# The MLP's second layer with activations as weights, and a scatter by blocks of 128 rows

## The chip, the cores and the metric

The kernel runs on one core of one Trainium2 chip. The metric is the device time of one execution in microseconds; lower is better. A profiled execution has a span, which goes from its first to its last instruction.

## What is computed

The reference has three stages in a row (cut to what matters):

```python
# attention: q, k, v [4, 12, 448, 64], RMS norm of q and k, softmax
# its output becomes x: 1792 tokens x 768
# moe: 8 experts, each takes 224 tokens; assignment is greedy over sorted logits
for e in range(E):
    h = np.maximum(x[mask] @ w1[e], 0.0)      # 768 -> 1024
    out[mask] = h @ w2[e]                     # 1024 -> 768
# cos MLP on all 1792 tokens
h = x @ w_in                                  # 768 -> 2048
g = h * np.cos(h)
return (g @ w_out).astype(np.float32)         # 2048 -> 768
```

`w_in` and `w_out` come as 64-bit floats. The kernel narrows them on the chip to pairs of 32-bit parts (hi, lo), which TensorE multiplies as float32r.

## The kernel before

**Order of work.** Every operation is put as a step into a `Plan` (lines 52 to 260), with the engines it may run on and an assumed cost; `Plan.run` then simulates the engines, chooses among available steps by due time (`late`, lowered by `rush`), and emits the program in that order. So a change of steps also changes the order of the others. A second plan, begun after the attention, holds the experts and the MLP.

**Routing.** Experts are found one after the other. `Router.phase` (line 1045) gives for one expert `idx`, a [112, 2] tile with the token numbers of its 224 rows in two halves, by products of one-hot rows `oh` with the digits `pv` of the token number (three digits, added by a reduce). For the third expert on it uses a search (`slow`, line 1003): SyncE writes `rows`, reads it back in eight broadcasts into `AB` (line 1014), and eight rounds of VectorE and TensorE (`ind`, `bd`) follow. GpSimd then gathers the expert's rows by an indirect DMA (line 1182).

**Groups.** Experts are taken in four pairs, `GROUPS`. For each pair both experts run, and leave 448 columns of activations, feature by feature, in `x2h` and `x2l`; then `mlp` (line 1304) does both layers for these 448 tokens. The route of the next pair's first expert is entered in the plan (`ahead`) in the middle of the second layer.

**MLP.** Layer one: 16 feature blocks f, each 6 x 3 matmuls of 448 columns (`three`: hi by hi, hi by lo, lo by hi), then the cosine on ScalarE and VectorE into `gh` and `gl`. Layer two: 6 output blocks d of 128 features, each 16 x 3 matmuls of 448 columns with w_out as weights. The result lies feature by feature, so ScalarE copies it to `o`, TensorE transposes it in four pieces of 112 tokens (into `tr`), VectorE copies these into `xo`, and after the last d four indirect DMAs (`scatter`, line 1349) write 112 rows each to the tokens' places, with `idx`. In the last group the last d is done in two halves of 224 columns. Weights come as 1 MB pieces through a ring of four buffers `wx` (`ready`, line 1236), all issued by SyncE (`SP`), which also issues the expert weights and the router's DMAs in program order.

**Narrowing.** `Narrow` (line 270) cuts w_in into 32 pieces and w_out into 24. 48 are narrowed during the attention and written to `w_in32`, `w_out32`; the last 8 of w_out, those of d = 4 and 5, are narrowed in group 0's second layer (`fresh`, line 1243), through `ws` and `na` into `wx`, and written out for the later groups.

Of the kernel before, what the change touches and what calls it, by code (L numbers as in the profile page):

```python
# [12 lines left out]
F32 = mybir.dt.float32  # L13
# [256 lines left out]
class Narrow:  # L270

    WIDE = {"wi": 3, "wo": 4}

    def __init__(self, nc, pairs):

        self.nc = nc
        self.todo, self.at = [], {}
        for tag, src, dst in pairs:
            s = src.bitcast(I32)
            for f in range(dst.shape[0]):  # L280
                n = self.WIDE[tag]
                for k in range(0, dst.shape[2], n):
                    w = s[k * 128:(k + n) * 128, f * 256:(f + 1) * 256].rearrange("(k p) c -> p k c", p=128)
                    self.at[tag, f, k] = len(self.todo)
                    self.todo.append((w, dst[f, :, k:k + n], f"{tag}{f}:{k}"))

    def piece(self, plan, i, raw, mag, parts=None):

        nc, v = self.nc, plan.vector
        src, dst, name = self.todo[i]  # L290
        n = dst.shape[1]
        r, a = raw[:, 0:n], mag[:, 0:n]
# [3 lines left out]
        plan.add([("SP", 0.46, lambda: nc.sync.dma_start(r, src))], [], [r], dma=0.36 * n, land=LAND)  # L296
# [7 lines left out]
        plan.add([("SP", 0.46, lambda: nc.sync.dma_start(dst, o.bitcast(F32)))], [o], [name], dma=0.36 * n)  # L304

    def plan(self, plan, pool, last):

        most = max(self.WIDE.values())
        raw = plan.ring(pool)("nr", 4, [128, most, 256], I32)
        mag = plan.ring(pool)("na", 2, [128, most, 128], I32)  # L310
        for i in range(last):
            self.piece(plan, i, raw(), mag())
# [412 lines left out]
class Router:  # L725
# [3 lines left out]
    def __init__(self, nc, pool, ident, L, rows):  # L729
# [76 lines left out]
        v.tensor_copy(io, tmp[0:CP, 272:272 + CP])  # L806
        pc = t("pc", [CP, NCOL, 3], BF16)
# [237 lines left out]
    def phase(self, idx, eid, first, quick):  # L1045
# [52 lines left out]
        nc.rush = rush  # L1098

# [30 lines left out]
TURN = 5  # L1130
# [5 lines left out]
def moe(tc, P, R, ident, x_rows, w1, w2, w_in, w_out, out, narrow):  # L1136

    nc = tc.nc
    with ExitStack() as ctx:
# [12 lines left out]
        obuf = ring("o", 1, [128, PT])  # L1152
# [3 lines left out]
        xf = cst.tile([128, KD, CAP], F32, name="xf")  # L1156
        xo = cst.tile([CP, 4, DM], F32, name="xo")
        mags = ring("na", MAGS, [128, 4, 128], I32)
# [3 lines left out]
        hT = gh[:, K1:K2]  # L1162
        gl = cst.tile([128, K2, PT], F32R, name="gl")
# [5 lines left out]
        def route(t, behind):  # L1169
# [3 lines left out]
            R.phase(idx[t], eid[t], t == 0, t in QUICK)  # L1173
# [62 lines left out]
        def ready(src, k0, n, keys):  # L1236

            x = parts()[:, 0:n]
            P.add([("SP", 0.46, lambda: nc.sync.dma_start(x.bitcast(F32), src[:, k0:k0 + n]))], keys, [x],
                  dma=n * 0.35)  # L1240
            return x[:, :, 0], x[:, :, 1]

        def fresh(d, k0):
            x = parts()
            for k in range(k0, k0 + K1, 4):
                i = narrow.at["wo", d, k]
                if i >= EARLY:
                    raw = stage().rearrange("p k n -> p (k n)").bitcast(I32).rearrange("p (k n) -> p k n", k=4)
                    narrow.piece(P, i, raw, mags(), x[:, k - k0:k - k0 + 4])
# [54 lines left out]
        def mlp(grp, ahead):  # L1304
            w = len(grp) * CAP
            for f in range(K2):
                hi, lo = ready(w_in[f], 0, KD, [f"wi{f}:{k}" for k in range(0, KD, narrow.WIDE["wi"])])
                p = acc()[:, 0:w]
                for d in range(KD):
                    block(lambda: three(p, hi[:, d], lo[:, d], x2h[:, d, 0:w], x2l[:, d, 0:w], d == 0, d == KD - 1))  # L1310
                r, k, a = rbuf()[:, 0:w], kbuf()[:, 0:w], gh[:, f, 0:w]
# [7 lines left out]
                P.either("tensor_tensor", gl[:, f, 0:w], r, a.bitcast(F32), op=ALU.subtract)  # L1319
            for d in range(KD):  # L1320
                if grp is GROUPS[0] and narrow.at["wo", d, 0] >= EARLY:
                    both = [fresh(d, k0) for k0 in range(0, K2, K1)]
                else:
                    both = [ready(w_out[d], k0, K1, [f"wo{d}:{k}" for k in range(k0, k0 + K1, narrow.WIDE["wo"])])
                            for k0 in range(0, K2, K1)]
                last = d == KD - 1
                if d == TURN:
                    ahead()
                cut = w // 2 if last and grp is GROUPS[-1] else w
                for a in range(0, w, cut):  # L1330
                    n, z = cut // CP, slice(a, a + cut)
                    p = acc()[:, 0:cut]
                    for f in range(K2):
                        hi, lo = (x[:, f % K1] for x in both[f // K1])
                        block(lambda: three(p, hi, lo, gh[:, f, z], gl[:, f, z], f == 0, f == K2 - 1))
# [4 lines left out]
                    g0 = a // CP  # L1340
                    v.tensor_copy(xo[:, g0:g0 + n, d * 128:(d + 1) * 128],
                                  q[0:CP, 0:n * 128].rearrange("p (g c) -> p g c", g=n))
                    for g in range(g0, g0 + n) if last else ():
                        P.add([("POOL", 1.07, lambda g=g: scatter(xo[:, g], idx[grp[g // 2]][:, g % 2:g % 2 + 1]))],
                              [xo[:, g]], [], dma=0.96)
# [22 lines left out]
        for grp in GROUPS:  # L1368
# [4 lines left out]
            behind = chain[-EARLIER]  # L1373
            mlp(grp, lambda: fetch(grp[-1] + 1, behind))
# [6 lines left out]
def kernel(  # L1381
# [22 lines left out]
    w_out32 = dram.tile([KD, 128, F2 // 128, 2, 128], F32, name="w_out32")  # L1404
    narrow = Narrow(nc, [("wi", w_in, w_in32), ("wo", w_out, w_out32)])
# [35 lines left out]
```

## Time and profile before

| | |
|---|---|
| median of 3 runs | 1161.94 us (1161.27 to 1163.94) |
| profiled execution | 1161.31 us, span 1159.4 us |
| granted TensorE clock, mean | 0.976 of full speed |
| busy: TensorE, VectorE, ScalarE, GpSimd | 1107.4, 895.6, 646.0, 134.2 us |
| attention | until about 340 us of the span |
| second layers of the MLP | about 520 to 581, 710 to 771, 900 to 961, 1086 to 1148 us |

The span is what the trace explains; the execution's own time lies 1.9 us above it.

### The profile page before, as it was taken

Reading aid. Unit: us, or ns where it says so; the run is one execution under the profiler, and the core shown is the slowest. Engines: PE = TensorE matmul, PEld = TensorE weight load, DVE = VectorE, ACT = ScalarE, POOL = GpSimd, SP = SyncE. Lnnn points to the kernel's source line nnn. Section 1 sums busy time; section 2 is a strip of 40 time slices with the busy share of each in tenths; the row PEclk is TensorE's granted clock in tenths of the full one; section 3 lists DMA queues with packets and bytes.
Section 4 is the critical chain, followed back from the end, with each engine's and each line's share of the span. In section 5 each row is a group of like instructions: output and inputs, shape, how many; then the busy total and the mean of one; then the engine's idle time right before and its main releaser. Section 6 shows DMA issues by size and latency. Waiting matters only on the chain.

```text
span 1159.4 us, 22182 instructions
## 1 busy us (share of the span) xinstructions
PE 1107.4 (96%) x7944; PEld 912.5 (79%) x7944; DVE 895.6 (77%) x2477; ACT 646.0 (56%) x1575; POOL 134.2 (12%) x288
## 2 busy tenths in 40 slices
PE   7999999999994999999999999999999999999996
PEld 4556666665553888999898899899899889999996
DVE  7878999999958888996997887578789577856401
ACT  4867888866552456763456564246666235746400
POOL 5432432331000000000001000001000000100001
PEclk9989999999995899999999999999999999999998
DMA  7236476565641489779579568838866956856761
GB/s 215 81 115 207 150 251 204 172 221 203 218 171 50 129 229 293 239 257 293 209 185 263 203 218 248 297 115 239 244 216 222 301 194 174 238 205 218 245 218 48
DMA packets 180814, 237.58 MB, mean 205 GB/s; under 512 B 14112, under 2 KB 156896, under 8 KB 175072
## 3 DMA queue, kind: packets, MB, share of 16 engines
q1 hardware_dynamic: 178144, 225.15, 61.4%
q0 software_dynamic: 2560, 11.01, 3.6%
q8 instruction: 62, 1.02, 0.4%
q14 instruction: 48, 0.39, 0.1%
HBM read 199.52 MB, written 36.52 MB: 204 GB/s over the span
## 4 chain that ended last, share of the span: by engine, by line
PE 36%; DVE 7%; DMA 6%; issue 1%; ACT 1%; SPq 0%; POOL 0%; POOLq 0%; ACTq 0%; DVEq 0%
PE acc L47 35%; DMA ws<-in_moe_w_dram 4%; DMA wx<-w_out 2%; DVE wx L47 2%; PE tr L47 1%; DVE r L47 1%; DVE oh L47 1%; ACT wx L1231 1%; DVE na L47 1%; DVE xo L47 0%; SPq L1014 0%; DMA rows<-vm 0%; DVE gl L47 0%; DVE xe L47 0%; POOL out_dram L1351 0%
## 5 line engine op out<-in xcount | busy, mean ns | idle before, releaser
L47 PE MATMUL acc<-gh,wx 128*128 128x448 f32 (+1 forms) x1568 | 360.7, 344 | 4.9 <-DVE gh L47 3.7
L47 PEld LDWEIGHTS acc<-gh,wx 128*128 128x128 f32 x1568 | 264.5, 189 | 23.5 <-DVE gh L47 6.0
L47 PE MATMUL acc<-x2h,wx 128*128 128x448 f32 x768 | 222.4, 368 | 0.0
L47 PEld LDWEIGHTS acc<-x2h,wx 128*128 128x128 f32 x768 | 144.7, 188 | 11.0
L47 PE MATMUL acc<-gl,wx 128*128 128x448 f32 (+1 forms) x400 | 143.2, 358 | 0.0
L47 PE MATMUL acc<-x2l,wx 128*128 128x448 f32 x384 | 140.3, 365 | 0.0
L47 DVE TENSOR_TENSOR wx<-ws,wx 128x768 fp32r<-128x768 f32 (+1 forms) x104 | 112.3, 1080 | 24.3 <-ACT wx L1231 22.1
L47 ACT ACTIVATE pf<-st 112x448 f32<-112x448 f32 x192 | 93.9, 539 | 50.4 <-PE st L47 49.8
L1231 ACT ACTIVATE wx<-ws 128x768 fp32r<-128x768 f32 (+1 forms) x104 | 97.7, 940 | 25.9 <-DMA ws<-in_moe_w_dram 14.0
L47 DVE TENSOR_REDUCE cm<-s 128x1 f32<-128x448 f32 x168 | 99.6, 618 | 12.5 <-PE s L47 10.1
L47 PE MATMUL acc<-xe,wx 128*128 128x448 f32 (+1 forms) x672 | 107.1, 320 | 0.5 <-DVE wx L47 0.5
L47 ACT ACTIVATE r<-r 128x448 f32<-128x448 f32 x128 | 74.1, 579 | 57.8 <-DVE r L47 56.0
L47 PEld LDWEIGHTS acc<-xe,wx 128*128 128x128 f32 x672 | 100.8, 189 | 5.4 <-DVE wx L47 0.8
L47 PE MATMUL st<-qq,kk 64*112 64x448 f32 x576 | 91.5, 397 | 1.9 <-ACT pf L47 1.9
L47 ACT ACTIVATE oh<-oh 128x896 bf16<-128x896 bf16 x48 | 45.6, 950 | 74.6 <-DVE oh L47 74.5
L1182 POOL DMA_INDIRECT xr<-x,idx x16 | 15.6, 977 | 588.1 <-issue 198.2
L47 PE MATMUL po<-pf,vr 112*64 112x448 f32 x384 | 83.1, 552 | 0.0
L47 PEld LDWEIGHTS acc<-gl,wx 128*128 128x128 f32 x400 | 75.5, 189 | 4.7
L47 PEld LDWEIGHTS acc<-x2l,wx 128*128 128x128 f32 x384 | 72.3, 188 | 5.2
L47 PEld LDWEIGHTS st<-qq,kk 64*112 64x112 f32 x576 | 49.3, 175 | 31.8 <-ACT pf L47 9.8
L47 ACT ACTIVATE sq<-qk 112x64 f32<-112x64 f32 (+1 forms) x195 | 57.2, 301 | 8.4 <-DVE rt L47 4.6
L47 DVE COPY xo<-tr 112x512 f32<-112x512 f32 (+1 forms) x25 | 16.6, 666 | 58.1 <-PE tr L47 56.4
(251 smaller groups left out, 1830.8 us busy)
## 6 DMA issues: line engine op xcount, KB each, us to landing
wx<-w_in SPq DMA_DIRECT2D x64, 768.0 KB
wx<-w_out SPq DMA_DIRECT2D x44, 1024.0 KB
ws<-in_moe_w_dram SPq DMA_DIRECT2D x64, 384.0 KB
ws<-in_moe_w_dram SPq DMA_DIRECT2D x48, 512.0 KB
nr<-in_moe_w_in_dram SPq DMA_DIRECT2D x32, 384.0 KB
w_in<-nr SPq DMA_DIRECT2D x32, 384.0 KB
nr<-in_moe_w_out_dram SPq DMA_DIRECT2D x16, 512.0 KB
w_out<-nr SPq DMA_DIRECT2D x16, 512.0 KB
```

The lines of the kernel that those rows point to most:

```text
L47: self.plan.add([(self.eng, self.plan.cost(self.eng, name, out, r, kw), lambda: f(*args, **kw), self.plan.shares(self.eng, name, out, r, k ...
L1182: P.add([("POOL", 2.1 - 0.9 * h, lambda x=x, h=h: nc.gpsimd.indirect_dma_start(out=x, out_offset=None, in_=x_rows, in_offset=bass.Indirect ...
L1231: P.add([("ACT", 0.093 + n * 0.1067, lambda: nc.scalar.activation(hi, s, AF.Copy)), ("DVE", 0.07 + n * 0.0667, lambda: nc.vector.tensor_co ...
```

## The change

The second layer is turned round. The activations `gh`, `gl` become the weights (128 rows of tokens a block), and w_out streams as the moving operand: first its 512 left columns, in 8 pieces of two feature blocks (`w_out32[0]`), then its 256 right ones, in 4 pieces of four (`w_out32[1]`). The output lies token by token, so it needs no transposes; it is evicted with a minus sign straight into `xo`, by ScalarE or VectorE.

448 rows are not a multiple of 128. Even groups put their columns at 64 to 511 of `gh` (`REST` = 64) and do three blocks (64 to 447); odd groups put theirs at 0 to 447 and do four (0 to 511), the last with the even group's remaining 64 rows. The scatter's indices, held in halves of 112 rows, must follow: `phase` also keeps the `digits`, and `place` shifts them to blocks of 128 by products with columns of a shifted unit matrix (`move`), adds the three digits and casts to `to`. The 8 pieces that are narrowed late are spread over the second layer.

```diff
 class Narrow:
-    WIDE = {"wi": 3, "wo": 4}
...
+        for tag, src, c0, dst, n in pairs:
...
+            blocks, per, m = dst.shape[0], dst.shape[2], dst.shape[4]
+            deep = src.shape[0] // 128
+            for b in range(blocks):
+                for i in range(0, per, n):
+                    k, c = divmod(b * per + i, deep)[::-1]
+                    w = s[k * 128:(k + n) * 128, 2 * (c0 + c * m):2 * (c0 + (c + 1) * m)]
+                    tile = (b + 8 * (tag == "wo1")) % 3 if i else -1
+                    self.todo.append(((tag != "wi") * (1 + (i > 0) + (tile > 0)), (tag, b, i), (
+                        w.rearrange("(k p) c -> p k c", p=128), dst[b, :, i:i + n], f"{tag}{b}:{i}")))
+        self.todo.sort(key=lambda t: t[0])
...
 class Router:   # setup
+        move = t("move", [CP, 288], BF16)
+        iota(tmp[0:CP, 16:304], [[1, 288]], base=-CP, step=-1)
+        v.tensor_scalar(move, tmp[0:CP, 16:304], 0.0, None, op0=ALU.is_equal)
+        v.tensor_scalar(t("tail", [128, 1]), row, 47.5, None, op0=ALU.is_ge)
...
-    def phase(self, idx, eid, first, quick):
+    def phase(self, idx, eid, first, quick, digits):
...
+        v.tensor_copy(digits, pi[0:CP, 0:6])
...
-TURN = 5
+TURN = 8
+REST = 64
...
-        obuf = ring("o", 1, [128, PT])
-        xo = cst.tile([CP, 4, DM], F32, name="xo")
+        xo = cst.tile([128, 4, DM], F32, name="xo")
-        gh = cst.tile([128, K2, PT], F32R, name="gh")
+        gh = cst.tile([128, K2, REST + PT], F32R, name="gh")
+        to = cst.tile([128, 7], I32, name="to")
+        sum3 = cst.tile([128, 7], F32, name="sum3")
+        digits = [cst.tile([CP, 6], BF16, name=f"dg{i}") for i in range(4)]
+        rest = cst.tile([CP, 3], BF16, name="rest")
...
+        def fresh(src, tag, b):
...
+                if at < EARLY:
+                    P.add([("SP", 0.46, lambda to=to, at=at: nc.sync.dma_start(to.bitcast(F32), narrow.todo[at][1]))],
+                          [narrow.todo[at][2]], [to], dma=1.45)
+                else:
+                    narrow.piece(P, at, stage().rearrange("p k n -> p (k n)").bitcast(I32), mags(), to)
...
         def mlp(grp, ahead):
...
-            for d in range(KD):
-                if grp is GROUPS[0] and narrow.at["wo", d, 0] >= EARLY:
-                    both = [fresh(d, k0) for k0 in range(0, K2, K1)]
...
-                    o, q = obuf()[:, 0:cut], turn()
-                    sc.activation(o, p, AF.Copy, scale=-1.0)
-                    for g in range(n):
-                        P.tensor.transpose(q[0:CP, g * 128:(g + 1) * 128], o[:, g * CP:(g + 1) * CP], ident)
...
+            starts, c0 = range(o, REST + PT - 64 * (1 - g % 2), 128), 0
+            for z, w in enumerate(w_out):
+                n, m = w.shape[2], w.shape[4]
+                ps = [acc()[:, 0:m] for _ in starts]
+                for k in range(0, K2, n):
+                    tag, b = f"wo{z}", k // n
+                    if g == 0 and narrow.late(tag, b, EARLY):
+                        hi, lo = fresh(w[b], tag, b)
+                    else:
+                        hi, lo = ready(w[b], narrow.keys(tag, b))
+                    if z and k == TURN:
+                        ahead()
+                    for s, p in zip(starts, ps):
+                        for i in range(n):
+                            f = k + i
+                            a, b = gh[:, f, s:s + 128], gl[:, f, s:s + 128]
+
+                            def f3():
+                                P.tensor.matmul(p, a, hi[:, i], start=f == 0, stop=False)
+                                P.tensor.matmul(p, b, hi[:, i], start=False, stop=False)
+                                P.tensor.matmul(p, a, lo[:, i], start=False, stop=f == K2 - 1)
+
+                            block(f3)
+                for i, p in enumerate(ps):
+                    y = xo[:, i, c0:c0 + m]
+                    P.add([("ACT", 0.05 + m / 1200.0, lambda y=y, p=p: nc.scalar.activation(y, p, AF.Copy, scale=-1.0)),
+                           ("DVE", 0.068 + m / 960.0, lambda y=y, p=p: nc.vector.tensor_scalar(y, p, -1.0, None,
+                                                                                              op0=ALU.mult))], [p], [y])
+                    if z:
+                        at = to[:, 3 * (g % 2) + i:3 * (g % 2) + i + 1]
+                        P.add([("POOL", 1.07, lambda i=i, at=at: scatter(xo[:, i], at))], [xo[:, i], at], [], dma=1.1)
+                c0 += m
+
+        def place(grp):
+
+            g, p, move = GROUPS.index(grp), turn(), R.P["move"]
+            odd = g % 2
+            half = [digits[t % 4][:, 3 * h:3 * h + 3] for t in grp for h in range(2)]
+            if odd:
+                v.tensor_scalar(rest, digits[(grp[0] - 1) % 4][:, 3:6], R.P["tail"][0:CP], None, op0=ALU.mult)
+            P.begin()
+            for b in range(3 + odd):
+                parts = [(half[n], CP * n - 128 * b) for n in range(4) if -CP < CP * n - 128 * b < 128]
+                if b == 3:
+                    parts.append((rest, 16))
+                for x, o in parts:
+                    P.tensor.matmul(p[:, 3 * b:3 * b + 3], move[:, CP - o:CP - o + 128], x, start=x is parts[0][0],
+                                    stop=x is parts[-1][0])
+            P.finish()
+            n = 3 * odd
+            v.tensor_reduce(sum3[:, n:n + 3 + odd], p[:, 0:9 + 3 * odd].rearrange("p (b k) -> p b k", k=3), AX.X, ALU.add)
+            v.tensor_copy(to[:, n:n + 3 + odd], sum3[:, n:n + 3 + odd])
...
             behind = chain[-EARLIER]
+            P.rush = 100.0
+            place(grp)
+            P.rush = 0.0
             mlp(grp, lambda: fetch(grp[-1] + 1, behind))
...
-    w_out32 = dram.tile([KD, 128, F2 // 128, 2, 128], F32, name="w_out32")
-    narrow = Narrow(nc, [("wi", w_in, w_in32), ("wo", w_out, w_out32)])
+    w_out32 = [dram.tile([F2 // 128 // n, 128, n, 2, 1024 // n], F32, name=f"w_out{n}") for n in (2, 4)]
+    narrow = Narrow(nc, [("wi", w_in, 0, w_in32, 3), ("wo0", w_out, 0, w_out32[0], 1),
+                         ("wo1", w_out, 512, w_out32[1], 2)])
```

## Rows read from the trace of the kernel before

**Rows 1.** The page: the span, and TensorE's busy time, share and instructions.

```profile
span 1159.4 us, 22182 instructions
PE 1107.4 (96%) x7944; PEld 912.5 (79%) x7944; DVE 895.6 (77%) x2477; ACT 646.0 (56%) x1575; POOL 134.2 (12%) x288
```

**Rows 2.** Windows, groups 0 and 2's second layers: length, busy (count), clock, DMA share, GB/s.

```profile
520.40:581.00 60.60, 60.23 (x329) 54.21 (x328) 48.69 (x138) 24.21 (x44) 2.09 (x2) 1.00 0.75 247
...
899.70:961.00 61.30, 60.49 (x330) 54.14 (x328) 39.21 (x133) 17.47 (x33) 1.90 (x2) 1.00 0.73 226
```

**Rows 3.** TensorE's waits, whole span: total us, times, longest.

```profile
PE tr L47 <- DVE xo L47: 1.7, 4, 0.6
```

**Rows 4.** Timeline, TensorE, group 3's second layer, 448 columns: start, us, operation.

```profile
1099.37 0.36 PE L47 MATMUL acc<-gl,wx 128*128 128x448 f32 x1
...
1118.22 0.37 PE L47 MATMUL acc<-gl,wx 128*128 128x448 f32 x1
```

**Rows 5.** Timeline, TensorE, group 3's last output block, 224 columns.

```profile
1141.80 0.27 PE L47 MATMUL acc<-gl,wx 128*128 128x224 f32 x1
...
1142.57 0.27 PE L47 MATMUL acc<-gl,wx 128*128 128x224 f32 x1
...
1144.91 0.27 PE L47 MATMUL acc<-gl,wx 128*128 128x224 f32 x1
1144.92 0.19 PEld L47 LDWEIGHTS acc<-gh,wx 128*128 128x128 f32 x1
```

**Rows 6.** The router's tile rt, group 2's second layer: duration ns, first and last start.

```profile
L47 PE MATMUL rt<-pv,oh x16: 168/192/193, 905.8 to 906.6; 112*112 112x6 bf16 x16
```

**Rows 7.** Timeline, VectorE, group 0's second layer: the cast into idx.

```profile
529.84 0.16 DVE L47 CAST idx<-row 112x2 int32<-112x2 f32 x1
```

**Rows 8.** Timeline, all engines, the end of the span.

```profile
1147.80 0.27 PE L47 MATMUL acc<-gh,wx 128*128 128x224 f32 x1
...
1148.39 0.36 ACT L47 ACTIVATE o<-acc 128x224 f32<-128x224 f32 x1 [2.42 <-PE tr L47]
...
1148.81 0.43 PE L47 MATMUL tr<-ident,o 128*112 128x128 f32 x2 [0.51 <-DVE xo L47]
1149.09 0.94 POOL L1351 DMA_INDIRECT out_dram<-xo,idx  x1 [150.13 <-DVE xo L47]
...
1152.82 0.94 POOL L1351 DMA_INDIRECT out_dram<-xo,idx  x1 [0.22 <-issue]
```

**Rows 9.** DMA issues: count, median us from issue to landing.

```profile
out_dram<-xo,idx POOLq DMA_INDIRECT x16, 6.5
```

**Rows 10.** Tile x2l, groups 0 and 2: the first and last start in layer one.

```profile
L47 PE MATMUL acc<-x2l,wx x96: 358/365/370, 461.0 to 519.9; 128*128 128x448 f32 x96
...
L47 PE MATMUL acc<-x2l,wx x96: 357/365/370, 840.5 to 899.3; 128*128 128x448 f32 x96
```

**Rows 11.** Timeline, SyncE's queue, group 2's second layer: issues, merged.

```profile
902.37 7.58 SPq L1014 DMA_DIRECT2D AB<-rows  x8
910.40 0.35 SPq L1239 DMA_DIRECT2D wx<-w_out  x1
```

**Rows 12.** Timeline, TensorE, group 2's second layer: its wait for weights.

```profile
920.84 0.47 PE L47 MATMUL acc<-gh,wx 128*128 128x448 f32 x1 [0.58 <-DMA wx<-w_out]
```

**Rows 13.** Timeline, SyncE's queue, group 0's second layer.

```profile
528.47 3.01 SPq L1239 DMA_DIRECT2D wx<-w_out  x2
```

**Rows 14.** Windows of 5 us, group 0's second layer (columns as in rows 2).

```profile
525.00:530.00 5.00, 5.00 (x38) 4.65 (x37) 4.87 (x25) 0.58 (x1) 0.00 (x0) 1.00 1.08 235
```

**Rows 15.** Tile na, the late narrowing, group 0: duration ns, first and last start.

```profile
L47 DVE TENSOR_SCALAR na<-na x16: 417/422/426, 461.1 to 562.2; 128x512 f32<-128x512 f32 x8, 128x512 int32<-128x512 int32 x8
L47 DVE SCALAR_TENSOR_TENSOR na<-ws,na x16: 683/688/694, 472.0 to 566.8; 128x512 int32<-128x512 int32 x16
...
L47 DVE TENSOR_TENSOR wx<-na,wx x8: 681/686/692, 545.1 to 568.9; 128x512 fp32r<-128x512 f32 x8
```

**Rows 16.** Timeline, GpSimd: the gather of the third expert's successor, expert four.

```profile
596.65 0.93 POOL L1182 DMA_INDIRECT xr<-x,idx  x1 [63.49 <-DVE sm L47]
```

More of the change, by code (lines that the diff above doesn't have):

```diff
@@ L270, with keys, late @@
 class Narrow:
-    WIDE = {"wi": 3, "wo": 4}
     def __init__(self, nc, pairs):
         self.nc = nc
-        self.todo, self.at = [], {}
-        for tag, src, dst in pairs:
+        self.todo = []
+        for tag, src, c0, dst, n in pairs:
             s = src.bitcast(I32)
[L280 to L285, printed above, removed]
+            blocks, per, m = dst.shape[0], dst.shape[2], dst.shape[4]
[8 more added lines that the diff above has]
+        self.todo.sort(key=lambda t: t[0])
+        self.at = {at: i for i, (_, at, _) in enumerate(self.todo)}
+        self.todo = [t for _, _, t in self.todo]
+    def keys(self, tag, b):
+        return [self.todo[i][2] for (t, x, _), i in self.at.items() if (t, x) == (tag, b)]
+    def late(self, tag, b, least):
+        return any(at >= least for (t, x, _), at in self.at.items() if (t, x) == (tag, b))
     def piece(self, plan, i, raw, mag, parts=None):
@@ L295, in piece @@
         low, high, f = words[:, :, :, 0], words[:, :, :, 1], a.bitcast(F32)
[L296 removed]
+        plan.add([("SP", 0.46, lambda: nc.sync.dma_start(r, src))], [], [r], dma=0.0028125 * n * m, land=LAND)
         plan.scalar.activation(f, high.bitcast(F32), AF.Abs)
@@ L1172, in route @@
             P.pad = 1.0 * (t > 1)
-            R.phase(idx[t], eid[t], t == 0, t in QUICK)
+            R.phase(idx[t], eid[t], t == 0, t in QUICK, digits[t % 4])
             P.ahead = P.pad = 0.0
@@ L1234, in weights, with ready @@
             return hi, lo
[L1236 to L1240, printed above, removed]
+        def ready(src, keys):
+            n, m = src.shape[1], src.shape[3]
+            x = parts().rearrange("p k h n -> p (k h n)")[:, 0:2 * n * m].rearrange("p (k h n) -> p k h n", k=n, h=2)
+            P.add([("SP", 0.46, lambda: nc.sync.dma_start(x.bitcast(F32), src))], keys, [x], dma=0.0028125 * n * m)
             return x[:, :, 0], x[:, :, 1]
[L1243 to L1249, printed above, removed]
+        def fresh(src, tag, b):
+            n, m = src.shape[1], src.shape[3]
+            x = parts().rearrange("p k h n -> p (k h n)")[:, 0:2 * n * m].rearrange("p (k h n) -> p k h n", k=n, h=2)
+            for (t, y, i), at in narrow.at.items():
+                if (t, y) != (tag, b):
+                    continue
+                to = x[:, i:i + narrow.todo[at][1].shape[1]]
+                if at < EARLY:
[3 more added lines that the diff above has]
+                    narrow.piece(P, at, stage().rearrange("p k n -> p (k n)").bitcast(I32), mags(), to)
             return x[:, :, 0], x[:, :, 1]
@@ L1304, in mlp @@
         def mlp(grp, ahead):
-            w = len(grp) * CAP
+            g = GROUPS.index(grp)
+            o = 0 if g % 2 else REST
             for f in range(K2):
-                hi, lo = ready(w_in[f], 0, KD, [f"wi{f}:{k}" for k in range(0, KD, narrow.WIDE["wi"])])
-                p = acc()[:, 0:w]
+                hi, lo = ready(w_in[f], narrow.keys("wi", f))
+                p = acc()[:, 0:PT]
                 for d in range(KD):
-                    block(lambda: three(p, hi[:, d], lo[:, d], x2h[:, d, 0:w], x2l[:, d, 0:w], d == 0, d == KD - 1))
-                r, k, a = rbuf()[:, 0:w], kbuf()[:, 0:w], gh[:, f, 0:w]
+                    block(lambda: three(p, hi[:, d], lo[:, d], x2h[:, d], x2l[:, d], d == 0, d == KD - 1))
+                r, k, a = rbuf(), kbuf(), gh[:, f, o:o + PT]
                 sc.activation(k, p, AF.Copy, scale=1.0 / (2.0 * math.pi))
@@ L1318, in mlp @@
                 sc.activation(a, r, AF.Copy)
-                P.either("tensor_tensor", gl[:, f, 0:w], r, a.bitcast(F32), op=ALU.subtract)
-            for d in range(KD):
-                if grp is GROUPS[0] and narrow.at["wo", d, 0] >= EARLY:
-                    both = [fresh(d, k0) for k0 in range(0, K2, K1)]
[L1323 to L1335, printed above, removed]
-                    o, q = obuf()[:, 0:cut], turn()
-                    sc.activation(o, p, AF.Copy, scale=-1.0)
-                    for g in range(n):
-                        P.tensor.transpose(q[0:CP, g * 128:(g + 1) * 128], o[:, g * CP:(g + 1) * CP], ident)
[L1340 to L1345, printed above, removed]
```

21 lines of the change are left out of this document (11 added, 10 removed).

## The prediction

> **What bounds the kernel now.** I read the page first. TensorE is busy for 1107.4 of 1159.4 us [rows 1], so the question is what TensorE issues and what it waits for; other engines count only where they make it wait. The change lies in the MLP, which runs four times, once for each pair of experts. Second, therefore, the windows of its second layers: each takes TensorE about 61 us, with 0.4 to 0.8 us of idle in it [rows 2]. VectorE is busy 48.7 us of the first of these stretches, where it also narrows the last weights and runs the router, and 39.2 us of the third; DMA engines are at 0.75 and 0.73. Third, TensorE's waits: all that the transposes of `tr` wait for is 1.7 us [rows 3]. So the kernel is bound by TensorE's instruction stream, and a change in that stream moves the end one for one, until another resource takes over in the shortened stretch. The sum therefore goes by TensorE's instructions, then its new waits, then the end.
>
> **Part 1, transposes removed.** Before, each of the 24 output blocks (6 for each of 4 groups) gets four transposes of 128 columns. In the narrow part at the end, two gl matmuls with nothing between them but their own triple are (1144.91 - 1142.57)/7 = 0.334 us apart; with a set of four transposes between they are 1142.57 - 1141.80 = 0.77 us apart [rows 5]. A set costs 0.436 us. 23.5 sets lie in the stream (the last two transposes belong to the end, part 4): -10.25 us. The 1.2 us that transposes wait inside the stream (1.7 [rows 3] less the 0.5 at the end [rows 8]) go too, and so does the ScalarE pass into `o` and VectorE's copy out of `tr`, which cost nothing on TensorE's path.
>
> **Part 2, other shapes.** The number of columns streamed is the same: two groups have 896 rows, which is 7 blocks of 128, and 7 x 16 x 3 x 768 = 2 x 288 x 448. But a matmul also costs something that doesn't go with its columns. 31 triples of 448 columns take 1118.22 - 1099.37 = 18.85 us, 0.2027 us a matmul [rows 4]; seven narrow triples give 0.1114 us for 224 columns [rows 5]. The line through both has 0.4076 ns a column and gives 0.1245 us at 256 and 0.2288 us at 512. Before: 1104 x 0.2027 + 96 x 0.1114 = 234.5 us. After: 6 + 8 = 14 blocks over four groups, 14 x 48 = 672 matmuls of each width, 672 x 0.3533 = 237.4 us: +2.9 us. [...] Lower bound: no extra cost, 0. I take +2.9, since both new widths lie next to a measured one. [...]
>
> **Part 3, the products with the shifted unit matrix.** `place` issues 6 products for an even group and 8 for an odd one, 28 in all, each bf16 with 3 columns. Nearest row: 16 products of 6 columns start within 0.8 us, 0.053 us each [rows 6]: 28 x 0.053 = +1.5 us (bounds: 0 if they fall into a wait; 28 x 0.192 = 5.4 if each cost its whole recorded duration). Their inputs, the `digits`, are ready a whole expert earlier, and `rush` puts them early, so I count no wait. At nothing: the copies into `digits`, `rest`, the reduce and the cast (some 20 small VectorE operations of about the 0.16 us of the cast into `idx` [rows 7], hidden behind matmuls; without that cover 3 us); `move` and `tail` in the setup (one iota, two VectorE operations, before the first route by hundreds of us); the new order of `narrow.todo` in the attention (same count, same elements); `TURN`, which only changes where the next route enters a plan that sorts by due time. Evictions go from six ScalarE passes and six VectorE copies a group to 6 or 8 passes on whichever is free: less work, off the path.
>
> **Part 4, the end.** Now the last real matmul starts at 1147.80 and ends 0.27 later. Then come the eviction at 1148.39 (0.36 us), transposes, copies, and only at 1149.09 the first of four scatters, 1.24 us apart, because the last column block completes all four together; the fourth starts at 1152.82 [rows 8] and lands 6.5 us later [rows 9], which is the end of the span. Tail: 1159.4 - 1148.07 = 11.3 us. After: a block of rows is complete when its own last 12 matmuls are, 12 x 0.1245 = 1.5 us before the next, which is more than 1.24, so the scatters no longer queue. The tail is the wait until the eviction (0.32), 256 columns (0.38), the step from a finished copy to the scatter (0.28: the copy that let TensorE go on at 1148.81 let the scatter start at 1149.09) and 6.5: 7.5 us. -3.8 us (bounds: -4.5 if the single scatter lands sooner, -2.5 if they still queue).
>
> **Part 5, new waits.** An even group now multiplies three blocks, an odd one four. A 1 MB piece of w_out32 lasts 18 x 0.2288 = 4.1 us in an even group, where it lasted 24 x 0.2027 = 4.9. Its deadlines move up. In group 2 the second layer starts at about 899.7 (last x2l matmul at 899.3 [rows 10], one more behind it). With four buffers, SyncE has issued four pieces by then; then come eight AB loads from 902.37 for 7.6 us, and the fifth piece only at 910.40 [rows 11]; TensorE waits 0.58 us for it, until 920.84 [rows 12]. After, the fifth piece is wanted at 899.7 + 4 x 4.12 + 0.85 (router products) = 917.0. If it lands when it did: 3.8 us, 3.2 more than before. Behind the AB loads stand every later w_out load and the next expert's; the sixth piece is wanted at 925 and should be there. Bounds: -0.6 (SyncE's order puts it before AB) and +4. In group 0 the fifth piece is issued at 528.47 [rows 13] while the DMA engines are at 1.08 [rows 14]; landing after the same 10.4 us it comes at 538.9, wanted at 520.3 (last x2l matmul at 519.9 [rows 10]) + 16.5 + 0.85 = 537.7: 1.2 us, and the eight pieces still to be narrowed now come from the second piece on, not at the end: I take +2 in all (0 to 8). Odd groups get slower per piece (5.5 us), so none there. The fourth accumulator of an odd group is needed 4.1 us after layer one, about when its cosine chain frees it; the plan can take other blocks: 0 (to +1 each).
>
> **Sum.** -10.25 - 1.2 + 2.9 + 1.5 - 3.8 + 3.2 + 2.0 = -5.65 us. Against the profiled execution's 1161.31 us (span 1159.4 [rows 1]) that is 1155.7; the median of the runs, 1161.94, is 0.6 above it: 1156.3 us.
>
> **Rivals.** *A, forecast:* 1156.3; its own range 1152.5 to 1159.6. *B, nothing new binds:* the plan moves the loads ahead of AB, or they land early; parts 1 to 4 stay and the old waits go: -10.85 - 0.6 gives 1150.5. For it: after 930 DMA engines have room again; against: a saturated stretch [rows 11 to 14] right at the deadlines. *C, group 0 takes the gain back, the other side:* its second layer should shrink from 61 to 144 x 0.3533 = 50.9 us, but VectorE has 48.7 us of work there [rows 2], of which the narrowing, now due early, is 8 x (2 x 0.42 + 2 x 0.69 + 0.69) = 23 us [rows 15]. It would push back the router's search, whose rows are gathered at 596.65 [rows 16] and land at 603, for an expert that now could start at about 601. Stretch no shorter: +8.1 over A, 1164.4; with the expert 4 us late too, 1168. It becomes slower than before when group 0 loses 8 us. For it: hardly a gap of VectorE; against: the evictions shrink, and the passes of the late pieces begin in layer one, from 461 on [rows 15]. *D, the change doesn't give narrow matmuls their rate:* a weight load is recorded with 0.19 us [rows 5]; if 256 columns could not go faster than that, 672 x 0.0635 = +42.7, 1199.0. Against: 224 columns run at 0.1114 with a load each, beside running matmuls. [...]
>
> **Chances and range.** A 0.50, B 0.22, C 0.25 (about 0.15 of it only back to no change, 0.09 slower), D 0.02, the rest small. Faster by over 0.2% (under 1159.6; 0.2% is what a measurement of this kernel can tell from no change) 0.74; within 0.2% 0.15; slower 0.11. The range reaches to B's value with a us beyond and into C: 1149.5 to 1164.0.
>
> **What would show it.** Part 1: no tr<-o rows. Part 2: 512 and 256 columns spaced 0.229 and 0.125 us. Even stretches some 51 us plus waits, odd ones 68. Part 3: 28 products at 0.05. Part 4: four scatters 1.5 us apart, the span ending 7.5 us after the last matmul. Part 5: a TensorE wait for wx<-w_out near the fifth piece of groups 0 and 2, 5 us in all; if that is under 1 us it is B, if idle and VectorE waits in group 0 pass 8 us it is C. Wrong would also be a different attention stage: it should keep its time within 1 us.

## The result, and the profile after

The changed kernel takes 1145.55 us (median of 4 runs, 1142.43 to 1146.25), the kernel before 1161.61 (4 runs, 1156.99 to 1163.94): a ratio of 0.9869 on record, interval 0.9845 to 0.9893 (the two medians alone give 0.9862). Two more measurements gave 0.9859 and 0.9850. The forecast, 1156.3 with a range from 1149.5, had the direction and missed the size by 10.8 us. The profiled execution (1146.25 us) has a span of 1144.5, 14.9 less than [rows 1], where the sum had 5.65.

The page of the changed kernel, its span and TensorE's part:

```profile
span 1144.5 us, 22358 instructions
PE 1098.1 (96%) x8020; PEld 892.8 (78%) x8020; DVE 883.0 (77%) x2472; ACT 645.6 (56%) x1578; POOL 138.2 (12%) x285
```

TensorE's busy time, as the profile models it, fell by 9.3 us against [rows 1]; the other 5.6 are waits and the end. To see where, I cut the span at the MLP's first layers, by the tile `x2l` as in [rows 10]. These are groups 0 and 1 of the changed kernel:

```profile
L47 PE MATMUL acc<-x2l,wx x96: 358/365/369, 459.2 to 518.2; 128*128 128x448 f32 x96
...
L47 PE MATMUL acc<-x2l,wx x96: 358/365/369, 639.6 to 698.8; 128*128 128x448 f32 x96
```

From the last such matmul of a group to the first of the next lie its second layer and the next two experts:

| us | layer one of group 0 starts | group 0 | 1 | 2 | 3, to the end |
|---|---|---|---|---|---|
| before | 461.0 | 131.2 | 130.5 | 128.9 | 73.4 |
| changed | 459.2 | 121.4 | 134.2 | 121.4 | 73.0 |

Even groups lost 9.8 and 7.5 us; of the odd ones, group 1 gained 3.7 and group 3 lost 0.4. That is the shape of three blocks of rows against four; the sizes are the question. Layer one of group 0 also starts 1.8 us earlier. TensorE's timeline in the changed kernel has both new widths. Here are gl matmuls of group 0 (256 columns) and group 2 (512 columns), and the new waits of both groups:

```profile
555.66 0.28 PE L47 MATMUL acc<-wx,gl 128*128 128x256 f32 x1
...
559.62 0.28 PE L47 MATMUL acc<-wx,gl 128*128 128x256 f32 x1
...
596.64 0.51 PE L47 MATMUL tr<-ident,xr 112*128 112x112 f32 x3 [1.44 <-DMA xr<-x,idx]
...
897.74 0.39 PE L47 MATMUL acc<-wx,gl 128*128 128x512 f32 x1
...
901.14 0.39 PE L47 MATMUL acc<-wx,gl 128*128 128x512 f32 x1
901.37 0.39 PE L47 MATMUL acc<-wx,gh 128*128 128x512 f32 x1
903.76 0.62 PE L47 MATMUL tr<-ident,xr 112*128 112x112 f32 x2 [2.00 <-DMA xr<-x,idx]
904.06 0.78 PE L47 MATMUL acc<-wx,gh 128*128 128x512 f32 x1
904.63 0.63 PE L47 MATMUL acc<-wx,gl 128*128 128x512 f32 x1
...
905.91 0.63 PE L47 MATMUL acc<-wx,gl 128*128 128x512 f32 x1
```

Eleven triples (three matmuls each, gl being one) of 256 columns take 559.62 - 555.66 = 3.96 us, 0.1200 us a matmul; five of 512 take 3.40 us, 0.2267. Then TensorE stands still for 2.0 us for the gathered rows of the next expert, and the triples behind that take 1.28 us instead of 0.68. The windows of 1 us there (TensorE, its loads, VectorE, ScalarE, GpSimd, clock, DMA share, GB/s) show the clock:

```profile
902.00:903.00 1.00, 0.00 (x0) 0.00 (x0) 0.00 (x0) 0.00 (x0) 0.00 (x0) 1.00 0.98 326
...
905.00:906.00 1.00, 1.00 (x4) 0.75 (x3) 0.00 (x0) 0.00 (x0) 0.00 (x0) 0.50 1.00 365
```

The granted clock falls from 1.00 to 0.50 behind the idle 2 us. TensorE's waits over the whole span, and SyncE's queue in group 2, to set against [rows 3, 11, 12]:

```profile
PE tr L47 <- DMA xr<-x,idx: 3.4, 2, 2.0
...
PE acc L47 <- DVE gh L47: 1.0, 3, 0.6
```

```profile
886.51 0.66 SPq L1261 DMA_DIRECT2D wx<-w_out  x1
888.64 4.46 SPq L1030 DMA_DIRECT2D AB<-rows  x8
893.48 4.55 SPq L1261 DMA_DIRECT2D wx<-w_out  x3
```

No wait for w_out is left, and neither of the two that were forecast came. The AB loads, which stood 2.7 us into group 2's second layer [rows 11], now stand about 4 us ahead of it. The end of the span, by the timeline:

```profile
1135.09 0.99 POOL L1405 DMA_INDIRECT out_dram<-xo,to  x1 [179.01 <-ACT xo L1373]
...
1138.43 0.28 PE L47 MATMUL acc<-wx,gh 128*128 128x256 f32 x1
...
1138.74 0.38 ACT L1373 ACTIVATE xo<-acc 128x256 f32<-128x256 f32 x1 [1.05 <-PE acc L47]
...
1139.40 0.96 POOL L1405 DMA_INDIRECT out_dram<-xo,to  x1 [0.38 <-ACT xo L1373]
```

From the last matmul's end, 1138.71, to the span's end are 5.8 us, where before they were 11.3 [rows 8] and the forecast said 7.5. The last scatter needs 1144.5 - 1139.4 = 5.1 us from its start to the end; before, 1159.4 - 1152.82 = 6.6. The time from the start of a scatter to its landing is only a part of that. These are the last four scatters before, and then of the changed kernel:

```profile
DMA to landing us min/median/max: 3.4/4.0/4.4
```

```profile
DMA to landing us min/median/max: 3.0/3.0/3.0
```

The span ends some 2.1 us after the last landing in both.

### The profile page after: what moved, and what is told of

The parts are those of the page before. It is cut to its first block, busy times and chain, and to the rows that moved or that the text cites. A ratio compares the mean times of both kernels' runs of the same rounds, so it can differ in the third digit from the quotient of the medians.

```text
span 1144.5 us, 22358 instructions
## 1 busy us (share of the span) xinstructions
PE 1098.1 (96%) x8020; PEld 892.8 (78%) x8020; DVE 883.0 (77%) x2472; ACT 645.6 (56%) x1578; POOL 138.2 (12%) x285
## 4 chain that ended last, share of the span: by engine, by line
PE 62%; DVE 16%; issue 13%; DMA 5%; ACT 3%; SPq 0%; POOL 0%; POOLq 0%; DVEq 0%; ACTq 0%
PE acc L47 39%; PE st L47 7%; PE po L47 5%; PE s L47 3%; PE dn L47 3%; PE t L47 3%; DVE na L47 2%; DVE r L47 2%; DVE oh L47 2%; DVE cm L47 2%; DMA ws<-in_moe_w_dram 1%; DMA xr<-x,idx 1%; PE rt L47 1%; DVE AB L47 1%; PE dn L444 1%
## 5 line engine op out<-in xcount | busy, mean ns | idle before, releaser
L47 PE MATMUL acc<-wx,gh 128*128 128x512 f32 (+1 forms) x896 | 228.3, 342 | 0.0
L47 PEld LDWEIGHTS acc<-wx,gh 128*128 128x128 f32 x896 | 156.4, 191 | 19.7 <-issue 1.2
L47 PE MATMUL acc<-wx,gl 128*128 128x512 f32 (+1 forms) x448 | 151.2, 338 | 0.0
L47 PE MATMUL acc<-gh,wx 128*128 128x448 f32 (+1 forms) x768 | 128.2, 324 | 1.4 <-DVE gh L47 1.0
L47 PEld LDWEIGHTS acc<-gh,wx 128*128 128x128 f32 x768 | 115.9, 191 | 8.8 <-DVE gh L47 2.2
L47 PEld LDWEIGHTS acc<-wx,gl 128*128 128x128 f32 x448 | 85.5, 191 | 8.3
L1203 POOL DMA_INDIRECT xr<-x,idx x16 | 21.3, 1330 | 517.0 <-issue 134.9
```

What stands on the lines that cost most here:

```text
L47: self.plan.add([(self.eng, self.plan.cost(self.eng, name, out, r, kw), lambda: f(*args, **kw), self.plan.shares(self.eng, name, out, r, k ...
L1203: P.add([("POOL", 2.1 - 0.9 * h, lambda x=x, h=h: nc.gpsimd.indirect_dma_start(out=x, out_offset=None, in_=x_rows, in_offset=bass.Indirect ...
```

## The experiments

Theory: fewer instructions in TensorE's stream (parts 1, 2 and 4) make the gain, more of it than forecast because three terms were mis-sized. Rival: something else moved, the plan's new order above all. Stages below are those of the table, groups 0 to 3.

**The changed kernel again**, as the measure for the others.

> The changed kernel itself, as the measure for the runs beside it. Both theories: the ratio to the kernel before that was seen, about 0.987, a profile of about 1144 us of span, two TensorE waits for gathered rows (xr) of about 1.4 and 2.0 us, no wait for w_out pieces.

It gave 1144.83 us, ratio 0.9859 (0.983 to 0.9887), stages 120.2, 134.2, 121.6, 72.9. Of the two waits for `xr` only that of group 2 came again (2.13 us).

**Part 1 by itself: the transposes put back, with nothing depending on them.** 24 sets of four transposes of a unit matrix into `tr` stand in the second layers' stream.

```diff
+                            dummy = turn() if s == starts[0] and f in (0, 6, 12) else None
                             def f3():
...
+                                for c in range(4 if dummy is not None else 0):
+                                    P.tensor.transpose(dummy[0:CP, c * 128:(c + 1) * 128], ident[:, 0:CP], ident)
```

> Each group's second layer of the changed kernel gets six sets of four transposes of the unit matrix into tr, inside its stream; nothing reads them. Theory 1 (part 1: a set costs 0.436 us of TensorE's stream, which bounds the kernel): 24 sets, +10.5 us over the changed kernel, 9.5 to 11.5. Rival (part of the transposes' cost before was hidden in other waits, so most of the gain came from somewhere else): less than 7 us.

1153.38 us (1151.81 to 1158.9), ratio 0.9945 (0.9926 to 0.9963): 8.6 us more than the changed kernel, between the two expectations. Groups 1 and 3, where nothing else moved much, took 137.1 and 75.7 us: +2.9 and +2.8 for six sets. Their second layers by themselves, from the first matmul to the last, grew by 2.5 and 2.7 us, 0.42 and 0.45 us a set (part 1 had 0.436). One set of group 3:

```profile
1109.79 0.39 PE L47 MATMUL acc<-wx,gl 128*128 128x512 f32 x1
...
1110.25 0.60 PE L47 MATMUL tr<-ident 128*112 128x128 f32 x4
...
1110.91 0.40 PE L47 MATMUL acc<-wx,gl 128*128 128x512 f32 x1
```

The two gl matmuls are 1.12 us apart, where 0.68 is usual: 0.44 us. Group 0 took 125.9, some 2 us beyond its six sets, which is not explained. Group 2 grew by 0.2 only, because its wait for gathered rows had gone: the rows' transposes stand later in TensorE's queue. The plan may have put them there because `tr` is shared again, or because the stretch is longer; the run doesn't separate the two, and in part 5's run, with `tr` free, they stand later as well.

**Part 2: is it the width or the arrangement?** The second layer's matmuls are trimmed to 7/8, then to 3/4, of their columns (1131.51 and 1122.48 us, one run each).

```diff
-                ps = [acc()[:, 0:m] for _ in starts]
+                used = m * 7 // 8
+                ps = [acc()[:, 0:used] for _ in starts]
...
-                                P.tensor.matmul(p, a, hi[:, i], start=f == 0, stop=False)
+                                P.tensor.matmul(p, a, hi[:, i, 0:used], start=f == 0, stop=False)
```

> The second layer's matmuls stream 448 of 512 and 224 of 256 columns; the left-out columns of xo hold zeros, so an eighth of each output row is not computed. Theory 1 (what a matmul costs beyond N/2400 ns depends on its width, as two points from before, 16.0 ns at 448 and 18.1 ns at 224, suggest): spacing in the second layer 0.2027 us and 0.1114 us again, also in the new arrangement. Theory 2 (the new arrangement, moving operand of 512 or 256 from wx and a [128, 128] weight from gh, has 13.3 ns whatever the width): 0.2000 and 0.1066 us. By theory 1 the four second layers last 672 x 0.3141 = 211.1 us, by theory 2 206.0.

> The second layer's matmuls stream 384 of 512 and 192 of 256 columns; the left-out columns of xo hold zeros, so a quarter of each output row is not computed. The trimming to 448 and 224 gave 0.202 and 0.112 us, 16 and 18 ns over N/2400, as in the old arrangement. If that extra grows as the matmul gets narrower (line through 448 and 224): 0.1766 and 0.0984 us, 16.6 and 18.4 ns. If it is 13.3 ns wherever the width is a multiple of 128: 0.1733 us at 384, and 192 shows 16 to 18.4 ns.

Timeline of the kernel with 7/8, gl matmuls of group 3:

```profile
1077.65 0.36 PE L47 MATMUL acc<-wx,gl 128*128 128x448 f32 x1
...
1085.55 0.37 PE L47 MATMUL acc<-wx,gl 128*128 128x448 f32 x1
...
1109.85 0.28 PE L47 MATMUL acc<-wx,gl 128*128 128x224 f32 x1
...
1113.87 0.28 PE L47 MATMUL acc<-wx,gl 128*128 128x224 f32 x1
```

The same of the kernel with 3/4:

```profile
1063.86 0.33 PE L47 MATMUL acc<-wx,gl 128*128 128x384 f32 x1
...
1067.50 0.33 PE L47 MATMUL acc<-wx,gl 128*128 128x384 f32 x1
...
1099.78 0.27 PE L47 MATMUL acc<-wx,gl 128*128 128x192 f32 x1
...
1103.80 0.27 PE L47 MATMUL acc<-wx,gl 128*128 128x192 f32 x1
```

Thirteen triples in 7.90 us, twelve in 4.02, seven in 3.64 and twelve in 4.02, together with the changed kernel's own. The granted clock was 1.00 in the windows of the changed kernel and of the kernel with 3/4; for the kernel with 7/8 its page has 0.9 or more in these slices. From 256 to 512 columns a matmul of the changed kernel grows by 0.2267 - 0.1200 = 0.1067 us, 0.4167 ns a column: that is the column time, which the expectations write as N/2400 (us for N columns).

| columns | 512 | 448 | 384 | 256 | 224 | 192 |
|---|---|---|---|---|---|---|
| us a matmul | 0.2267 | 0.2026 | 0.1733 | 0.1200 | 0.1117 | 0.1117 |
| ns over 0.4167 a column | 13.3 | 15.9 | 13.3 | 13.3 | 18.3 | 31.7 |

448 and 224 cost in the new arrangement what they cost in the old [rows 4, 5], 0.2026 and 0.1117 us against 0.2027 and 0.1114: the width decides, not the arrangement. 512, 384 and 256 lie on one line with 13.3 ns over the column time. 192 takes as long as 224, so 224 lies on a floor of about 0.112 us, and not on that line; 448 lies 2.6 ns above it, and why is open. Neither expectation had the 31.7 ns at 192. What the floor is, no run here shows.

**Part 4: 112 rows or the queue?** First, scatters of 112 of each block's 128 rows, issued when those of the changed kernel are.

```diff
-                        P.add([("POOL", 1.07, lambda i=i, at=at: scatter(xo[:, i], at))], [xo[:, i], at], [], dma=1.1)
+                        P.add([("POOL", 1.07, lambda i=i, at=at: scatter(xo[0:CP, i], at[0:CP]))], [xo[:, i], at], [], dma=1.1)
```

> Every scatter writes 112 rows of its 128, so 16 rows of each block are never written. Theory 1 (the scatters of before landed late, 6.5 us, because a transfer of 112 rows moves more slowly): landing goes back towards 6.5 us, from 3.3, and the last microseconds of the span move 267 GB/s or less, with a tail of 7 us or more behind the last matmul. Theory 2 (before they landed late because four were issued back to back, 1.24 us apart, while each needs more than that): landing stays near 3.0 to 3.3 us, since the issues stand 1.44 us apart as in the changed kernel, and the tail stays near 5.8 us.

Its last issue and two windows of 1 us at the end, the second its best, and then two of the changed kernel from the same part of its end:

```profile
1138.53 0.94 POOL L1405 DMA_INDIRECT out_dram<-xo,to  x1 [0.41 <-ACT xo L1373]
...
1135.90:1136.90 1.00, 1.00 (x11) 1.00 (x10) 0.00 (x0) 0.38 (x1) 0.81 (x2) 1.00 0.79 252
...
1139.90:1140.90 1.00, 0.00 (x0) 0.00 (x0) 0.00 (x0) 0.00 (x0) 0.00 (x0) 1.00 0.90 292
```

```profile
1136.50:1137.50 1.00, 1.00 (x11) 1.00 (x10) 0.00 (x0) 0.19 (x1) 0.97 (x1) 1.00 0.93 393
1137.50:1138.50 1.00, 1.00 (x11) 1.00 (x9) 0.00 (x0) 0.19 (x1) 0.62 (x3) 1.00 0.48 197
```

Its span ends at 1144.9, 6.4 us after its last scatter starts and 7.1 after its last matmul, with an eighth fewer bytes (one run, 1146.72 us). Its DMA engines are busy for about as long in their best microsecond and move less: 0.90 for 292 GB/s against 0.93 for 393. Its last scatters land 3.9 to 4.3 us after their start, where the changed kernel's take 3.0 and those of before 3.4 to 4.4:

```profile
DMA to landing us min/median/max: 3.9/4.1/4.3
```

So the tail is as theory 1 had it, and theory 2's 5.8 is out. Theory 1's 267 GB/s and its landing of 6.5 us are out too: over all 14 scatters the median is 4.3 us, where the changed kernel has 3.3. The 6.5 of before [rows 9] is a median over all 16, of which 12 lie in the middle of the span; why those landed later still, in the middle, was not tested.

Second, all four of the last group's scatters held until the fourth block is evicted, by a GpSimd copy of one element of that block ahead of each. Two earlier versions (1140.69 and 1142.53 us in one run each) entered the scatters ahead of the later evictions, so that three of the four left as in the changed kernel, and they told nothing.

```diff
+                        send = lambda i=i, at=at: P.add([("POOL", 1.07, lambda: scatter(xo[:, i], at, g == 3))],
+                                                        [xo[:, 0:4], at], [], dma=1.1)
...
+                for send in later:
+                    send()
```

> Third version of the held scatters (the two earlier ones entered them ahead of the later evictions, so three of the four left on time as before): the four of the last group now stand behind all four evictions. If a scatter of 128 rows needs less than the time between two issues, nothing queues: the last one still ends 5.1 us after its start, and the tail is eviction 0.4 + copy 0.4 + three issues 1.3 to 1.5 apart + 5.1 = 10.2 us, against 5.8. If back-to-back issue is itself what made the scatters of before late, the last ends 6.4 us or more after its start: tail 11.5 or more.

```profile
1137.19 1.00 POOL L1414 DMA_INDIRECT out_dram<-xo,to  x1 [0.60 <-issue]
...
1141.61 0.98 POOL L1414 DMA_INDIRECT out_dram<-xo,to  x1 [0.16 <-issue]
```

The span ends at 1146.7 (one run, 1148.49 us), 5.1 us after the last start: scatters of 128 rows don't queue at 1.47 us apart, and the last one's bytes have moved within 3.1 us of its start:

```profile
1142.70:1143.70 1.00, 0.00 (x0) 0.00 (x0) 0.00 (x0) 0.00 (x0) 0.00 (x0) 0.50 0.62 258
1143.70:1144.70 1.00, 0.00 (x0) 0.00 (x0) 0.00 (x0) 0.00 (x0) 0.00 (x0) 0.50 0.33 135
1144.70:1145.70 1.00, 0.00 (x0) 0.00 (x0) 0.00 (x0) 0.00 (x0) 0.00 (x0) 0.50 0.00 0
```

The tail is 10.8 us, where 10.2, or over 11.5 with a queue, were expected. The last eviction began at 1135.89, so holding costs 5 us of tail, as the last stage says (78.0 against 73.0). So the rows make the time from the last start to the end (6.4 against 5.1), and issuing each block as it is done saves the rest. The queue has a part in it where the rows are 112: of the four at the end of before, 1.24 us apart, the first landed after 3.4 us and the last after 4.4. By itself a scatter of 112 rows took 0.4 us longer than one of 128, then, and 1.0 us came with the three ahead of it.

**Part 5: the forecast wait.** Expert 7's `rows` is held until group 2's layer one is over, which puts AB back to about where it stood before.

```diff
+        if self.gate is not None:
+            nc.steps[-1].after[self.gate] = True
...
+                    R.gate = gates[2] if t == 7 else None
```

> The last router search's write of its rows is held until layer one of group 2 ends, so its eight AB loads stand where they stood before the change, some 2.7 us into the second layer; nothing else is edited. Theory 1 (the forecast's price of 3.8 us was right for that position, and only the position moved, to 4 us before the second layer): TensorE waits 2 to 4 us for a w_out piece in group 2, near 17 us into the stretch, and the time is 2 to 5 us over the changed kernel's. Rival (an even group has slack for the fifth piece wherever AB stands): no such wait over 0.6 us and the time within 1 us.

```profile
893.24 7.01 SPq L1032 DMA_DIRECT2D AB<-rows  x8
902.54 1.57 SPq L1263 DMA_DIRECT2D wx<-w_out  x2
...
909.11 0.47 PE L47 MATMUL acc<-wx,gh 128*128 128x512 f32 x1 [2.17 <-DMA wx<-w_out]
```

AB now stands some 3.6 us into the second layer. The wait comes, for the piece issued behind AB, with 2.2 us instead of the 3.8 worked out. But it stands in place of the wait for `xr`, which is gone from this second layer: that takes 57.4 us, where the three profiles of the changed kernel have 58.0, 58.1 and 56.3. The stages are 120.9, 134.8, 123.1 and 72.9; the 1.5 more in group 2 than in the changed kernel's second run lie behind the second layer, where a wait of 1.1 us for `xr` comes instead. The total, 1144.44 us, ratio 0.9846 (0.9822 to 0.9869), resolves none of that. So it is shown that the position of AB makes this wait, and not that the kernel would have been slower by it. For group 0 no such run was made; there AB moved too, from 523.22, 3 us into the second layer, to 3 us ahead of it:

```profile
515.65 4.93 SPq L1030 DMA_DIRECT2D AB<-rows  x8
```

**The new wait.** The plan assumes that a gather lands after 5 us. With 9, it puts the transposes of gathered rows later.

```diff
-                    land=5.0)
+                    land=9.0 if t >= 2 else 5.0)
```

This is the last version; the first has 9 for all experts, the second for experts 6 and 7 only.

> The plan assumes that gathered rows land 9 us after the gather, not 5, so their transposes enter TensorE's queue later; nothing else is edited. Theory 1 (the new waits in groups 0 and 2 are transposes of gathered rows that stand in TensorE's queue before the rows have landed, and the 2.0 us wait also drops the clock to 0.50 for 3 us): the xr waits fall from 3.4 to under 1 us, the clock stays at 1.00 after 900 us, and the time is 4 to 5 us lower than the changed kernel's. Rival (the stretch is short of DMA, so whatever comes next waits instead): the wait moves to wx<-w_out pieces or expert weights and the time stays within 1 us.

> The gathers of experts 6 and 7 alone are planned to land after 9 us, not 5. If the wait for xr and the lower clock behind it are what group 2 loses (2.1 us of wait at 901, and clock 0.50 for 3 us, 1.8 us): stage of group 2 118.3 to 118.5 us instead of 121.6 (as in the run with all gathers later), the others as in the changed kernel's second run (120.2, 134.2, 72.9), layer one of group 0 starting where it did, total 3 us less: about 1141.5 us, ratio 0.983. Rival: the wait only moves to another operand (wx for the fifth piece, since TensorE arrives earlier): stage of group 2 stays within 1 us of 121.6 and the ratio at 0.986.

> The gathers of experts 2 to 7 are planned to land after 9 us, those of experts 0 and 1 after 5 as before. If what the run with all gathers later lost was lost ahead of group 0's layer one by experts 0 and 1 (4 us later start, 61.0 instead of 59.0 us for the layer): stages 118.2, 134.5, 118.3, 73.0 and group 0's layer one from 457 to 459, total 4.5 us less than the changed kernel: about 1140 us, ratio 0.982. Rival: the loss belongs to run-to-run spread of the attention or to the new order of the whole plan: no difference from the changed kernel, 0.986, with the wait for wx taking the place of that for xr.

> The changed kernel itself, beside the version with later gathers from expert 2 on and on the same chip: 0.986 of before as in its two earlier measurements (0.9869, 0.9859), stages 120 to 121.5, 134.2, 121.5, 73.0 us.

> The version with the gathers of experts 2 to 7 planned to land after 9 us, a second time. If its 0.9834 against 0.9859 and 0.9869 is real: 2.5 to 4 us less than the changed kernel beside it on the same chip, all of it in group 2's stage (117.6 against 121.5). Rival: spread of the runs: within 1.5 us of the changed kernel.

| gathers later | us | ratio | stages |
|---|---|---|---|
| none (the changed kernel) | 1144.87 | 0.9850 (0.9828 to 0.9872) | 121.0, 134.4, 120.8, 73.0 |
| all | 1146.52 | 0.9868 (0.9843 to 0.9893) | 118.2, 134.9, 118.3, 73.0 |
| experts 6, 7 | 1142.12 | 0.9849 (0.9821 to 0.9877) | 119.4, 134.2, 118.7, 72.9 |
| from 2 on | 1139.67 | 0.9834 (0.9813 to 0.9855) | 120.5, 133.9, 117.6, 73.0 |
| from 2 on, again | 1145.01 | 0.9824 (0.98 to 0.9848) | 123.0, 134.3, 117.9, 72.9 |

In group 2 the theory holds: the wait for `xr` is gone, and the stage is 2.1 to 4.0 us shorter in all four. The granted clock stays at 1.00 from 880 to 915 us in the version with experts 6 and 7 and in the first run of that from 2 on; with all gathers later the triples behind the wait of 1.57 us for `wx` stand 0.68 to 0.70 us apart again, not 1.28; for the second run from 2 on no window shows it. In group 0 it doesn't hold: with later gathers from expert 2 on its stage takes 120.5 and 123.0. Its rival is half right, since a wait for `wx` takes its place (2.40 us with experts 6 and 7, 1.06 from 2 on):

```profile
896.11 0.50 PE L47 MATMUL acc<-wx,gh 128*128 128x512 f32 x1 [2.40 <-DMA wx<-w_out]
```

But layer one of group 2 takes 60.0 us in these versions instead of 59.1, group 0's up to 61.0, and the totals don't separate: all intervals overlap, and on the one chip where both ran, the medians are 1144.87 and 1145.01, not the 2.5 to 4 us less that were expected. That this version beats the changed kernel is not shown.

## Why the prediction was wrong in size

**Part 1 was right.** 0.436 us a set was forecast; the experiment gives 0.42 to 0.45 us, and where before has a set between matmuls of 448 columns these stand 1.05 us apart instead of 0.61.

**Part 2 failed at "The line through both has 0.4076 ns a column".** One of its two points, 224, lies on a floor (192 takes the same time), and the other is 2.6 ns off the line of 512, 384 and 256. The term should have been 672 x (0.2267 + 0.1200) - 234.5 = -1.5 us, not +2.9: 4.4 us of the miss. "Since both new widths lie next to a measured one" was no protection. The lower bound, 0, allowed no gain.

**Part 3 was nearly right.** The eight products of group 3 lie between two triples:

```profile
1042.64 0.36 PE L47 MATMUL acc<-x2l,wx 128*128 128x448 f32 x1
...
1043.05 0.33 PE L47 MATMUL tr<-dg,move 112*128 112x3 bf16 x7
1043.24 0.16 PE L47 MATMUL tr<-rest,move 112*128 112x3 bf16 x1
...
1043.55 0.36 PE L47 MATMUL acc<-x2l,wx 128*128 128x448 f32 x1
```

The next x2l comes 0.91 us after the last, where a triple takes 0.61: 0.30 us for eight, some 1.1 for 28 where 1.5 was forecast.

**Part 4 had the mechanism and mis-sized "and 6.5".** It read "and lands 6.5 us later [rows 9], which is the end of the span". The scatter that started at 1152.82 landed after 4.4 us, and the span ended 2.2 us behind that; that the sum of the two equals the median landing of all 16 scatters is luck. Both 4.4 and 6.5 belong to scatters of 112 rows; the last one of 128 rows landed after 3.0 us, and the span ended 5.1 us after its start. Besides, the last eviction starts 0.03 us after its matmul, not 0.32. The tail shrank by 5.5 us, not 3.8: 1.7 of the miss.

**Part 5 failed at "If it lands when it did".** AB no longer stands in the middle of the w_out loads: SyncE goes on with them at 893.48, 1 us into the layer, where before it did so at 910.40, 10.7 us into it [rows 11]. What in the plan brought AB forward was not traced. Where AB is put back in group 2 the wait appears, with 2.2 us. That is rival B's mechanism, loads that land early, whose time, 1150.5, still held part 2's and part 4's sizes; with them corrected it is 1144.4. Why no wait came in group 0 was not tested. 5.2 us of forecast waits are missing. Besides, the old waits for gh (3.7 to 1.0 us) and wx (0.9 to 0), which the sum left in place, are gone: 3.6. Against that stand the new wait for `xr`, 3.4 us over the span, with about 1.6 of lower clock behind it in this execution (two triples at 1.28 instead of 0.68 us and a slow start of the first), and two new waits of the router's `ind` matmuls in group 0's second layer, 0.43 and 0.63 us. These waits vary: the other two profiles of the changed kernel have 2.1 and 3.3 us for `xr`, 1.4 and 2.1 for gh.

**The account.** -5.65 - 4.4 - 0.4 - 1.7 - 5.2 - 3.6 + 5.0 + 1.1 = -14.85. The measured -14.9 looks the same, but 1.8 of it lies ahead of group 0's layer one, which starts at 459.2 instead of 461.0, and no term is about that stretch. What is to be compared is 13.1, so the account takes off 1.8 us too much; where they went is open. Whether the attention, which the new order of the narrowing also touches, took part in the gain is open too: three profiles of the changed kernel start that layer at 455.0, 457.6 and 459.2, and before has one profile.

**The rivals.** C did not happen: group 0's stretch shrank by 9.8 us. The step it named is there, though: TensorE waits 1.44 us at 596.64 for the gathered rows of the next expert, and in the second profile not at all. D did not: 256 columns run at 0.1200 us, each with a load of its own (8020 loads for 8020 matmuls by the page); it was nearer than it looked, though, since the floor lies only 0.008 us below. (D's 0.0635 us goes with a load of 0.188 us; with the 0.19 of its row it is 0.0655, and 44 us instead of 42.7.) The range stopped at 1149.5 because it took B's waits with part 2's and part 4's likeliest values, instead of their favourable bounds too.

## What to carry to other kernels

Before extrapolating a matmul's cost over its width, look for a third point: two points can lie on two different limits, and here the narrower one lay on the floor of about 0.112 us. When an edit shortens a stretch of a planned kernel, work the sum out with the other queues both where they stand and where the plan would put them; the waits then forecast are conditional on that order, and they belong to a rival, not in the sum. When a plan moves a stage earlier, look whether it then arrives ahead of its data, as the transposes of gathered rows do here. And a median over all transfers of a kernel is not the time of its last one: read that one by itself.

## What was not expected of the hardware

A scatter of 112 rows took 6.4 us from its start to the span's end, one of 128 rows 5.1: more rows, and sooner done, at 393 GB/s against 292 in the best microsecond of each. Why is not settled.

The same wait of about 2 us for `xr` in group 2 has different costs. In the first two profiles of the changed kernel, with 2.00 and 2.13 us, the granted clock fell to 0.50 behind it, for some 3 us; in the third, with a wait of 1.92 us, it stayed at 1.00:

```profile
896.00:900.00 4.00, 2.08 (x11) 1.47 (x10) 0.00 (x0) 0.00 (x0) 0.00 (x0) 1.00 1.03 332
900.00:904.00 4.00, 4.00 (x19) 3.25 (x19) 0.00 (x0) 0.00 (x0) 0.00 (x0) 1.00 1.04 328
```

Group 2's second layer took 58.0 and 58.1 us with the fall and 56.3 without it; the whole stage differs by less, 121.4 and 121.6 against 120.8, because a later wait for gh is longer in the third profile (1.45 us). The version with held scatters that took 1142.53 us even had 2.68 us of this wait without a fall (1.00 from 896 to 908 us). So in this kernel the wait costs its own time in each profile, and in some about 1.7 us more; what decides between the two was not found.
